# Two of the first four pairs of head groups by column tiles, and a planner with other transfer times

## The chip, the cores and the metric

The kernel runs on one core of one Trainium2 chip. The metric is the time of one execution on the device in microseconds, as the median of several runs; lower is better.

## The reference

Two layers, each of them attention with a compressive memory followed by a feed-forward network, on one sequence of 2048 tokens with 640 features. Both layers use the same weights. All inputs are bf16.

```python
x = x + attention(layernorm(x)); x = x + relu(layernorm(x) @ w1) @ w2      # twice, w1: 640 x 1728

def attention(x):                       # 32 heads of 20 features, 4 segments of 512 tokens
    q, k, v = x @ wq, x @ wk, x @ wv    # split into heads and segments
    M, z = 0, 0
    for s in range(4):
        a_dot = softmax(q_s k_s^T * 20**-0.5 + causal_mask) v_s
        a_mem = (phi(q_s) M) / (phi(q_s) z + 1e-6)      # phi(t) = t + 1 if t > 0 else exp(t)
        o_s = sigmoid(beta) * a_mem + (1 - sigmoid(beta)) * a_dot
        M, z = M + phi(k_s)^T v_s, z + sum(phi(k_s))
    return concat(o) @ wo
```

## The kernel before

The program is not written in the order in which it runs. `plan()` describes the work as generators ("streams"), each of which yields operations with a cost in ns, with what they wait for and with the buffer that they need. `Sched.run` places one operation after the other: it takes, among the heads of all streams, the one that can start first by the planner's own times (a delay called `late` can be added, and a priority settles ties). Each engine then gets its instructions as one fixed list, with waits on semaphores, and works through it in order. So a wrong time in the planner costs nothing by itself: it only makes an order in which an instruction stands ahead of others that could have run. `plan()` is built for each of several switch costs in `STARTS`, which differ by 0.75 ns, and the plan is taken whose order gives the smallest sum of four passes of `Sched.late`, a replay of the order in which transfers land late at random.

The numbers that the planner uses for transfers: an issue time, bytes divided by a rate, and a latency `lat` (`dma`, `ld`, `turn`, `late_loads`). `PE_MARGIN`, `TRUST_NS` and `JOIN_NS` are margins on waits of PE. `keep_busy` puts products with the identity (L627, "fillers") in front of an instruction where the planner expects PE to wait for long.

The work, by (layer `a`, segment `s`), eight times:

- `lnorm`/`ln_b`: statistics (L651) and normalization on DVE, the power -1/2 on POOL (L665), then a transpose by DMA (`turn`, L671, issued from SP's queue, which it holds while it is issued). The first segment is transposed on PE instead (L728).
- `proj_part`, `proj_v`: products for K, Q (into `stg`, feature by feature) and V (into `v_aug`, token by token, with a column of ones for each head).
- `spill`, `fill`: K and Q go to DRAM (`scr`) and come back as `pad`, four heads at partitions 0, 32, 64 and 96. For the first pair `first_heads` copies `stg` to `pad` directly.
- `scores` (L1103): a *pair* `m` is two groups of four heads; there are 32 pairs, four in each segment. Scores of four heads run in row tiles, in up to five rounds of two halves (the buffers X and Y). `exps` (L1155) turns them into `PT` on ACT, `causal` (L1167) clears above the diagonal on POOL.
- `apply`: the values of a pair, in one of two ways. *By token* (`values_by_token`, L1197): `PT` is the stationary operand and 21 columns of V move, 40 products for each group of four heads; DVE divides straight from PSUM (L1209, L1210, L1213) into `o_sb`. *By column tiles* (L1246): V is stationary in four column tiles and `PT` moves, 16 products for each group; the result is features by tokens, so it is evicted to `av` (L1254 on DVE or L1255 on ACT), transposed by DMA to `avt` (`turn_av`) and then divided (`divide`, L1282, L1283, L1290).
- `combine`, `turn_o`, `out_proj`: the memory's part is added, `o_sb` is transposed by DMA to `oT`, and `wo` is applied.
- `ffn`: 65 products of 512 columns with `w1`, then 112 products with `w2`, 320 columns wide.

Which pairs go by token is set here; four pairs make a segment, so this is pairs 0 to 3:

```python
BY_TOKEN = ((0, 0),)                               # segments
LATER = range(len(BY_TOKEN) * G // 2, NSEG * G)    # pairs that go through turn_av and divide
```

Of the kernel before, what the change touches and what calls it, by code (L numbers as in the profile page):

```python
# [14 lines left out]
NSEG = 4  # L15
# [3 lines left out]
FC = D // 128  # L19
# [138 lines left out]

LONE_NS = 300.0
SWITCH_NS = 97.0  # L160
STARTS = [SWITCH_NS + 0.75 * (k - 32 // 2) for k in range(32)]
LATE_NS = 300.0
JOIN_NS = 4000.0
SEM_NS = 60.0
PE_MARGIN = 80.0
IDLE_NS = 300.0
COLD_NS = 8000.0
TRUST_NS = {"dma": 1000.0, "pool": 400.0, "act": 400.0, "dve": 400.0, "pe": 0.0}
HOLDERS = 1
# [3 lines left out]
class Sched:  # L173
# [93 lines left out]
    def run(self):  # L267
        while True:
# [22 lines left out]
            for prio, n, st, alts, op, late in heads:  # L291
                ok = []
                if op.mode == "cols" and self.pe_mode == "full" and not self.streams[0][4]:
                    since = max([self.at(t) for t in op.waits], default=0.0)
                    late = max(0.0, JOIN_NS - max(0.0, alts[0][1] - since)) if alts else 0.0
                if prio > 0 and alts and alts[0][3] == "pe":
                    sl = self._pick(op.acq).tks if op.acq is not None else []
                    sure = max([self.at(t) + TRUST_NS[self.P.lane(t)] for t in op.waits + sl], default=0.0)
                    late = max(late, sure - alts[0][1])
                for end, start, k, e in alts:  # L300
                    if not any(p2 < min(prio, HOLDERS) and st2 is not st
                               and any(e2 == e and s2 + HOLD_TOL[e] < end for _, s2, _, e2 in al2[:1])
                               for p2, _, st2, al2, _, _ in heads):
# [31 lines left out]
            if op.dma is not None:  # L335
                tk = self.P.dma(e, fns[0][0], op.dma)
                self.dma_free = max(self.dma_free, start + 300.0) + tail[1]
                self.t[(id(tk[0]), tk[1])] = max(self.dma_free, end) + tail[0]
                if tail[2]:
                    self.free[e] = max(end, self.dma_free)  # L340
                out = tk
            else:
                marks = []
                for fn, mark in fns:
                    tk = self.P.op(e, fn, mark)
                    if tk is not None:
# [6 lines left out]
    def late(self, seed):  # L353

        rnd = random.Random(seed)
        free = {e: 800.0 for e in ENGS}
        t = {}
        dma_free = 0.0
        for e, hold, tail, waits, out, is_dma in self.log:
            m = SEM_NS + (PE_MARGIN if e == "pe" else 0.0)  # L360
            start = max([t[id(k[0]), k[1]] + m for k in waits], default=0.0)
            start = max(free[e], start)
            free[e] = start + hold
            if is_dma:
                dma_free = max(dma_free, start + 300.0) + tail[1]
                land = max(dma_free, free[e]) + tail[0] + rnd.expovariate(1.0 / LATE_NS)
                if tail[2]:
                    free[e] = max(free[e], dma_free)
            else:
                land = free[e] + tail  # L370
            for k in out:
                if k is not None:
                    t[id(k[0]), k[1]] = land
        return max(t.values())
# [33 lines left out]
def plan(switch, sb, sem_, psum, dram, A_x, A_wq, A_wk, A_wv, A_wo, A_beta, B_x, B_w1, B_w2, out):  # L408
# [84 lines left out]


    def ld(e, name, nbytes, fn, waits=()):
        tk = yield dma(e, sem_("d_" + name), nbytes, fn, waits, lat=2200.0)
        S.set(name, tks=[tk])

    def wload(e, name, w, src, waits=()):
# [24 lines left out]
    def late_loads():  # L524
# [27 lines left out]
        for n, (name, nbytes, fn) in enumerate(pieces):  # L552
            if name not in sems:
                sems[name] = sem_("d_" + name)
            w = yield Need("ex", *divmod(n, 5))
            if n == n2:
                v0 = yield Need("v00")
                q1 = yield Need("q01")
                w2w = v0 + q1 + early_done
            tk = yield dma("sp", sems[name], nbytes, fn, w[:1] + (w2w if n >= n2 else []) + z1, issue=400.0, lat=4500.0)  # L560
            left[name] -= 1
            if left[name] == 0:
                S.set(name, tks=[tk])
# [101 lines left out]
        tk = yield pool(760, lambda e: e.tensor_tensor(rstd[:, sl], lnU[:, sl], mhalf[:, 0:n], ALU.pow), [tk] + h)  # L665
        return tk

    def turn(slot_sem, dst, src, waits):

        n = src.shape[-1] // 128  # L670
        tk = yield dma("sp", slot_sem, 32768 * n, lambda e: e.dma_start_transpose(dst, src), waits,  # L671
                       issue=max(1400.0, 140.0 * n), lat=2000.0, rate=270.0, holds=True)
        return tk

    def lnorm(s, x_tks, pool_, parts=1):
# [3 lines left out]
        for p0 in range(0, 4, n):  # L679
# [11 lines left out]
            for i in range(p0, p0 + n, 2):  # L691
                t = 4 * s + i
                nm = lambda e, bx, t, k: e.tensor_scalar(
                    bx.ap[:, k * D:k * D + D], x_sb[:, t + k, :], mv[:, t + k, 0:1], rstd[:, t + k:t + k + 1],
                    ALU.subtract, ALU.mult)
                bx, t0 = yield dve(D, 4, lambda e, bx, t=t: nm(e, bx, t, 0), [tch], extra=120, acq=XN)
                t1 = yield dve(D, 4, lambda e, bx=bx, t=t: nm(e, bx, t, 1), [tch], extra=120)
                tT = yield from turn(xn_sem[id(bx)], xt.ap[:, i * FC:(i + 2) * FC, :], bx.ap, [t0, t1] + xt.tks)
                bx.release(tT)
                done.append(tT)  # L700
        return xt, done
# [474 lines left out]

        return 32 if (g, hh) != (G - 1, 3) else DH + 1

    BY_TOKEN = ((0, 0),)

    def values_by_token(m, a, s, g0, vt):

# [44 lines left out]
    def apply(m):  # L1227
# [30 lines left out]
        S.set("av", m, tks=[sl] + ev)  # L1258
        yield from done_values(a, s, g0, tk)

    LATER = range(len(BY_TOKEN) * G // 2, NSEG * G)

    def turn_av(m):
        ev = yield Need("av", m)
        sl, ev = ev[0], ev[1:]
        at = yield Acq([AVT])
        tT = yield from turn(avt_sem, at.ap, sl.ap.rearrange("p z t -> p (z t)"), ev + at.tks)
        sl.release(tT)
        S.set("avt", m, tks=[at, tT])

# [52 lines left out]
    def turn_o(a, s):  # L1323
        ow = yield Need("oseg", a, s)
        turned = []
        for k in range(2):
            ot = yield Acq([OT[k]])
            ot.users = []
            tT = yield from turn(ot_sem[id(ot)], ot.ap, o_sb[:, 2 * k:2 * k + 2, :].rearrange(
                "p i d -> p (i d)"), ow + ot.tks)  # L1330
            turned.append(tT)
            S.set("oT", a, s, k, tks=[ot, tT])
        OSB.release(*turned)
# [17 lines left out]
    def ln_b(p):  # L1351
        def f(a, s):
# [21 lines left out]
            tT = yield from turn(xn_sem[id(bx)], xt.ap[:, 2 * p * FC:(2 * p + 2) * FC, :], bx.ap, tn + xt.tks)  # L1374
            bx.release(tT)
            S.set("hx", a, s, p, tks=[tT])
        return f
# [188 lines left out]
```

## Time and profile before

| | |
|---|---|
| runs | 565.68, 567.0, 568.76 us; median 567.0 us |
| profiled execution | 565.3 us, of which the span of instructions is 563.5 us |
| granted clock of TensorE | 1.00 |
| values by token | 320 products (8 groups of 40) |
| values by column tiles | 896 products (56 groups of 16) |
| fillers (L627) | 66 products |
| transposes `avt<-av` | 28 |

In the rows of the profile, a *group* is line, engine, operation, what is written and read, shapes and count, then busy time, mean duration and idle time before. A row of the *timeline* is a start, a duration, the instruction with its count, and in brackets how long the engine had been idle and what ended that. Products overlap in PE's pipeline, so what one costs is the distance from its start to the next start and not its duration.

### The profile page before, as it was taken

What the parts mean: (1) busy time and instruction counts of PE and PEld (TensorE: products, weight loads), DVE (VectorE), ACT (ScalarE), POOL (GpSimd) and SP (SyncE); (2) the same over time, 40 slices, a digit from 0 to 9 for tenths busy, and PEclk for the clock granted to TensorE, in tenths of its full rate; (3) what the DMA queues carried; (4) which work ended last, traced back from release to release, by engine and by line L of the source; (5) the groups of instructions that cost most, each with busy time, mean ns of one, the idle gap of its engine ahead of it and who ended that gap; (6) DMA issues with size and microseconds to landing.
All of it is one profiled execution on the core that took longest, in us unless ns stands there. A gap on an engine that the chain in (4) does not pass through costs nothing.

```text
span 563.5 us, 12875 instructions
## 1 busy us (share of the span) xinstructions
PE 556.4 (99%) x5219; PEld 305.0 (54%) x5219; DVE 420.1 (75%) x1070; ACT 404.2 (72%) x512; POOL 195.1 (35%) x302
## 2 busy tenths in 40 slices
PE   8999999999999999999999999999999999999998
PEld 7664555445554454645446544555445654665655
DVE  6989789888999689878898997688747964560202
ACT  4789998987788878778986688778878678113140
POOL 4544344333344335444433443035322433110000
PEclk9999999999999999999999999999999999999999
DMA  8695988383474136542375131880326410512101
GB/s 268 120 221 138 238 218 182 74 224 56 97 171 94 44 88 159 118 95 72 92 163 115 27 66 26 193 148 20 67 80 173 109 43 20 116 45 48 47 1 47
DMA packets 130109, 60.93 MB, mean 108 GB/s; under 512 B 108930, under 2 KB 119938, under 8 KB 130050
## 3 DMA queue, kind: packets, MB, share of 16 engines
q1 hardware_dynamic: 129830, 59.85, 45.5%
q8 instruction: 41, 0.67, 0.5%
q10 hardware_dynamic: 220, 0.26, 0.2%
q14 instruction: 18, 0.15, 0.1%
HBM read 20.57 MB, written 12.85 MB: 59 GB/s over the span
## 4 chain that ended last, share of the span: by engine, by line
PE 87%; DVE 8%; DMA 2%; ACT 1%; SPq 1%; issue 0%
PE ps L643 56%; PE ps L640 11%; PE ps L1103 8%; PE ps L1246 6%; DVE stats L651 2%; PE ps L996 2%; PE ps L1197 1%; PE ps L1047 1%; DVE x_sb L1317 1%; PE ps L1394 1%; DMA avt<-av 1%; DVE xn_tok L705 1%; SPq L913 1%; DMA oT<-o_sb 1%; ACT PT L1155 1%; DVE stg L816 1%
## 5 line engine op out<-in xcount | busy, mean ns | idle before, releaser
L1155 ACT ACTIVATE PT<-ps 128x1024 bf16<-128x1024 f32 x320 | 310.0, 1022 | 70.3 <-PE ps L1103 64.6
L1167 POOL TENSOR_SCALAR_AFFINE_SELECT PT<-PT 128x512 bf16<-128x512 bf16 x256 | 166.6, 668 | 268.2 <-ACT PT L1155 267.9
L643 PE MATMUL ps<-w_r,hT 128*128 128x320 bf16 (+2 forms) x768 | 123.0, 299 | 0.0
L643 PE MATMUL ps<-xnT,w_r 128*128 128x512 bf16 x416 | 113.3, 379 | 0.0
L1317 DVE TENSOR_TENSOR x_sb<-x_sb,ps 128x320 bf16<-128x320 bf16 (+1 forms) x128 | 60.3, 479 | 66.7 <-PE ps L643 66.0
L643 PEld LDWEIGHTS ps<-w_r,hT 128*128 128x128 bf16 x768 | 72.4, 98 | 31.9 <-issue 4.4
L1425 ACT ACTIVATE hT<-ps 128x512 bf16<-128x512 f32 x55 | 32.7, 598 | 50.0 <-PE ps L643 49.7
L1103 PE MATMUL ps<-pad 20*128 20x128 bf16 (+3 forms) x1024 | 64.8, 301 | 1.6 <-ACT PT L1155 0.9
L643 PEld LDWEIGHTS ps<-xnT,w_r 128*128 128x128 bf16 x416 | 39.7, 98 | 44.0 <-issue 3.2
L651 DVE BATCH_NORM_STATS2 stats<-x_sb 128x6 f32<-128x320 bf16 x126 | 56.4, 472 | 2.1 <-DMA x_sb<-in_A_x_dram 1.8
L1254 DVE CAST av<-ps 128x512 bf16<-128x512 f32 x53 | 36.2, 684 | 14.8 <-PE ps L1246 14.7
L1103 PEld LDWEIGHTS ps<-pad 20*128 20x128 bf16 x1024 | 18.3, 92 | 52.6 <-ACT PT L1155 25.6
L643 PE MATMUL ps<-wo_r,oT 128*128 128x320 bf16 x256 | 46.1, 299 | 0.0
L1246 PE MATMUL ps<-PT,v_aug 128*32 128x256 bf16 (+5 forms) x896 | 40.7, 302 | 0.0
L1423 DVE TENSOR_SCALAR hT<-ps 128x512 bf16<-128x512 f32 x49 | 33.4, 683 | 9.1 <-PE ps L643 9.0
L640 PE MATMUL ps<-xnT,w_r 128*128 128x512 bf16 x104 | 39.6, 380 | 0.0
L643 PE MATMUL ps<-wv_r,xnT 128*128 128x320 bf16 x192 | 36.7, 300 | 0.0
L643 PE MATMUL ps<-xnT,wk_r 128*128 128x512 bf16 (+1 forms) x140 | 36.1, 349 | 0.0
L643 PE MATMUL ps<-xnT,wq_r 128*128 128x512 bf16 (+1 forms) x140 | 34.9, 349 | 0.0
L665 POOL TENSOR_TENSOR rstd<-lnU,mhalf 128x2 f32<-128x2 f32 (+2 forms) x25 | 20.8, 831 | 38.0 <-DVE lnU L661 34.4
L816 DVE CAST stg<-ps 128x512 bf16<-128x512 f32 (+1 forms) x48 | 29.5, 618 | 3.3 <-PE ps L643 3.2
L1290 DVE TENSOR_TENSOR o_sb<-avt,rden 128x320 bf16<-128x320 bf16 x56 | 30.5, 562 | 0.6
(117 smaller groups left out, 695.8 us busy)
## 6 DMA issues: line engine op xcount, KB each, us to landing
pad<-scr SPq DMA_DIRECT2D x124, 80.0 KB
scr<-stg SPq DMA_DIRECT2D x34, 256.0 KB, 2.9
out_dram<-x_sb SPq DMA_DIRECT2D x15, 160.0 KB, 1.8
w_r<-in_B_w_dram SPq DMA_DIRECT2D x10, 216.0 KB, 4.2
w_r<-in_B_w_dram SPq DMA_DIRECT2D x13, 160.0 KB, 2.8
x_sb<-in_A_x_dram SPq DMA_DIRECT2D x9, 160.0 KB, 2.8
scr<-w_r SPq DMA_DIRECT2D x5, 256.0 KB, 3.6
x_sb<-in_A_x_dram SPq DMA_DIRECT2D x3, 320.0 KB, 7.2
```

The costliest lines, as they stand in the source:

```text
L640: bk, tk = yield pe(mm_ns(n), [(lambda e, bk, a=a, b=b: e.matmul(bk.ap[:, 0:n] if len(b.shape) == 2 else bk.ap[:, 0:n].rearrange("p (i n) ...
L643: tk = yield pe(mm_ns(n), [(lambda e, k=k, a=a, b=b, bk=bk: e.matmul(bk.ap[:, 0:n] if len(b.shape) == 2 else bk.ap[:, 0:n].rearrange("p (i ...
L651: tk = yield dve(320, 1, lambda e, c2=c2: e.bn_stats(stats6[:, t, c2, :], x_sb[:, t, c2 * 320:(c2 + 1) * 320]), xt)
L816: te = yield evac(N, 1, lambda e, sg=sg, bk=bk: e.tensor_copy(sg.ap[:, t0:t0 + N], bk.ap[:, 0:N]), lambda e, sg=sg, bk=bk: e.activation(sg ...
L1103: fns.append([(lambda e, z=z, j=j, hh=hh, N=N, o=o, sl=sl: e.matmul(ps[:, hh, o:o + N], sl.ap[32 * hh:32 * hh + DH, z, 0, 128 * j:128 * j ...
L1155: tx = yield act(1024, lambda e, dst=dst, src=src: e.activation(dst, src, ACT.Exp, scale=SCALE), sc + pw)
L1167: tm = yield pool(600.0, lambda e, reg=reg: e.affine_select(out=reg, in_=reg, pattern=[[0, 4], [1, 128]], compare_op=ALU.is_ge, fill=0.0, ...
L1246: fns.append((lambda e, bk, j=j, hh=hh, pt=pt, g=g0 + z: e.matmul(bk.ap[32 * hh:32 * hh + wide(g, hh), 128 * j:L], VAUG[vx(a, s)][:, j].re ...
L1254: te = yield evac(L, 1, lambda e, sl=sl, z=z, bk=bk: e.tensor_copy(sl.ap[:, z], bk.ap), lambda e, sl=sl, z=z, bk=bk: e.activation(sl.ap[:, ...
L1317: ta = yield dve(n, 1, lambda e: e.tensor_tensor(x_sb[:, t, c0:c0 + n], x_sb[:, t, c0:c0 + n], bk.ap[:, 0:n], ALU.add), [tk] + list(waits) ...
L1423: th = yield evac(512, 1, lambda e, dc=dc, bk=bk: e.tensor_scalar(hT[:, dc, :], bk.ap[:, :], 0.0, None, ALU.max), lambda e, dc=dc, bk=bk: ...
L1425: lambda e, dc=dc, bk=bk: e.activation(hT[:, dc, :], bk.ap[:, :], ACT.Relu), [tk] + HT.tks)
```

## The change

Pairs 0 and 1 get their values by column tiles, pairs 2 and 3 stay by token. The planner's latencies are set for each transfer by itself; two margins are added: an operation on ACT or DVE that waits for a transfer is planned as if the transfer ended 800 ns later (`SURE_NS`), and transfers issued between 8 and 106 us are given 600 ns more (`EARLY_NS`). The replay that chooses among plans delays those transfers too and adds 1 us after a long wait of PE (`COOL_NS`), and 48 plans are built instead of 32. All lines after the constants move down by up to 11; the diff:

```diff
-STARTS = [SWITCH_NS + 0.75 * (k - 32 // 2) for k in range(32)]
+STARTS = [SWITCH_NS + 0.75 * (k - 48 // 2) for k in range(48)]
+SURE_NS = 800.0
+EARLY_NS = 600.0
+LOADS_NS = 106e3
+COOL_NS = 1000.0
...
@@ Sched.run
+                if alts and alts[0][3] in ("act", "dve"):
+                    sure = max([self.at(t) for t in op.waits if self.P.lane(t) == "dma"], default=0.0)
+                    late = max(late, sure + SURE_NS - alts[0][1])
...
-                self.t[(id(tk[0]), tk[1])] = max(self.dma_free, end) + tail[0]
+                self.t[(id(tk[0]), tk[1])] = max(self.dma_free, end) + tail[0] + (EARLY_NS if 8e3 < start < LOADS_NS else 0.0)
@@ Sched.late
+            if e == 'pe' and start - free[e] > 800.0 and start > 10e3:
+                start += COOL_NS
...
+                if 8e3 < start < LOADS_NS:
+                    land += rnd.expovariate(1.0 / EARLY_NS)
@@ plan
-        tk = yield dma(e, sem_("d_" + name), nbytes, fn, waits, lat=2200.0)
+        tk = yield dma(e, sem_("d_" + name), nbytes, fn, waits, lat={"x0a": 1950.0, "x0b": 1950.0, "x01": 1500.0, "wk0": 2900.0, "wq0": 2900.0, "wk1": 2900.0, "wq1": 2500.0, "wv": 2200.0, "x10": 3800.0, "x11": 3800.0}.get(name, 2200.0))
...
-            tk = yield dma("sp", sems[name], nbytes, fn, w[:1] + (w2w if n >= n2 else []) + z1, issue=400.0, lat=4500.0)
+            tk = yield dma("sp", sems[name], nbytes, fn, w[:1] + (w2w if n >= n2 else []) + z1, issue=400.0, lat=3500.0)
...
-    def turn(slot_sem, dst, src, waits):
+    def turn(slot_sem, dst, src, waits, lat=2000.0):
...
-                       issue=max(1400.0, 140.0 * n), lat=2000.0, rate=270.0, holds=True)
+                       issue=max(1400.0, 140.0 * n), lat=lat, rate=270.0, holds=True)
...
-    BY_TOKEN = ((0, 0),)
+    BY_TOKEN = (2,3)
...
-        if (a, s) in BY_TOKEN:
+        if m in BY_TOKEN:
...
-    LATER = range(len(BY_TOKEN) * G // 2, NSEG * G)
+    LATER = [m for m in range(NSEG * G) if m not in BY_TOKEN]
...
@@ turn_av: lat=1600.0;  turn_o, lnorm and ln_b: lat=2400.0
```

More of the change, by code (lines that the diff above doesn't have):

```diff
@@ L697, in lnorm @@
                 t1 = yield dve(D, 4, lambda e, bx=bx, t=t: nm(e, bx, t, 1), [tch], extra=120)
-                tT = yield from turn(xn_sem[id(bx)], xt.ap[:, i * FC:(i + 2) * FC, :], bx.ap, [t0, t1] + xt.tks)
+                tT = yield from turn(xn_sem[id(bx)], xt.ap[:, i * FC:(i + 2) * FC, :], bx.ap, [t0, t1] + xt.tks, lat=2400.0)
                 bx.release(tT)
@@ L1266, in turn_av @@
         at = yield Acq([AVT])
-        tT = yield from turn(avt_sem, at.ap, sl.ap.rearrange("p z t -> p (z t)"), ev + at.tks)
+        tT = yield from turn(avt_sem, at.ap, sl.ap.rearrange("p z t -> p (z t)"), ev + at.tks, lat=1600.0)
         sl.release(tT)
@@ L1329, in turn_o @@
             tT = yield from turn(ot_sem[id(ot)], ot.ap, o_sb[:, 2 * k:2 * k + 2, :].rearrange(
-                "p i d -> p (i d)"), ow + ot.tks)
+                "p i d -> p (i d)"), ow + ot.tks, lat=2400.0)
             turned.append(tT)
@@ L1373, in f @@
                 tn.append(tk)
-            tT = yield from turn(xn_sem[id(bx)], xt.ap[:, 2 * p * FC:(2 * p + 2) * FC, :], bx.ap, tn + xt.tks)
+            tT = yield from turn(xn_sem[id(bx)], xt.ap[:, 2 * p * FC:(2 * p + 2) * FC, :], bx.ap, tn + xt.tks, lat=2400.0)
             bx.release(tT)
```

## The prediction

> **What bounds the kernel now.** I read the page first, for the engine that is busy for the whole span:
>
> ```profile
> span 563.5 us, 12875 instructions
> PE 556.4 (99%) x5219; PEld 305.0 (54%) x5219; DVE 420.1 (75%) x1070; ACT 404.2 (72%) x512; POOL 195.1 (35%) x302
> PEclk9999999999999999999999999999999999999999
> ```
>
> PE is busy 99% of the span, at one clock throughout. But a busy PE can be a waiting one, so I read PE's timeline next, for the distance from one start to the next in dense stretches and for bracketed idle time.
>
> ```profile
> 8.04 1.00 PE L627 MATMUL ps<-ident 128*128 128x128 bf16 x15
> 8.88 0.27 PE L640 MATMUL ps<-xnT,wk_r 128*128 128x256 bf16 x1
> 8.98 0.60 PE L643 MATMUL ps<-xnT,wk_r 128*128 128x256 bf16 x4
> 9.42 0.44 PE L728 MATMUL ps<-ident,xn_tok 128*128 128x128 bf16 x5
> 9.70 0.27 PE L640 MATMUL ps<-xnT,wq_r 128*128 128x256 bf16 x1
> ...
> 18.41 0.27 PE L640 MATMUL ps<-xnT,wk_r 128*128 128x256 bf16 x1
> 19.30 0.40 PE L1103 MATMUL ps<-pad 20*128 20x512 bf16 x4 [0.62 <-DMA pad<-stg]
> ...
> 84.00 0.31 PE L640 MATMUL ps<-wo_r,oT 128*128 128x320 bf16 x1 [0.21 <-DMA oT<-o_sb]
> ...
> 94.88 0.39 PE L1103 MATMUL ps<-pad 20*128 20x512 bf16 x2 [0.27 <-ACT PT L1155]
> 99.50 0.40 PE L1103 MATMUL ps<-pad 20*128 20x512 bf16 x4 [0.20 <-ACT PT L1155]
> 100.11 0.31 PE L640 MATMUL ps<-wv_r,xnT 128*128 128x320 bf16 x1 [0.22 <-DVE av L1254]
> 166.41 0.40 PE L1103 MATMUL ps<-pad 20*128 20x384 bf16 x8 [0.44 <-ACT PT L1155]
> 195.96 0.34 PE L996 MATMUL ps<-BD,stg 128*128 128x84 bf16 x3 [0.23 <-DVE om_sb L1007]
> 555.48 1.79 PE L643 MATMUL ps<-w_r,hT 128*128 128x320 bf16 x12
> 557.11 0.30 PE L643 MATMUL ps<-w_u,hL 128*128 128x320 bf16 x1
> ```
>
> The last two rows are the pace when nothing is in the way: 12 products 320 wide in 557.11 - 555.48 = 1.63 us, 0.136 us each. Five 256 wide take 9.42 - 8.88 = 0.54 us, 0.109 each. The bracketed waits shown are the larger ones after the start; together 0.62 + 0.21 + 0.27 + 0.20 + 0.22 + 0.44 + 0.23 = 2.19 us. So PE is bound by its own list of instructions. A change can win what it takes off that list and about 2 us of waits; it loses what its new order makes PE wait.
>
> **The change part by part.**
>
> *Values of pairs 0 and 1.* Four groups of 40 narrow products (two pairs of two head groups) become four groups of 16 products in column tiles. Both kinds are in the trace, and so is a burst of scores:
>
> ```profile
> 28.62 1.16 PE L1197 MATMUL ps<-w_r,PT 128*128 128x21 bf16 x40
> 29.64 0.30 PE L640 MATMUL ps<-wv_r,hT 128*128 128x320 bf16 x1
> ...
> 96.30 0.30 PE L640 MATMUL ps<-wv_r,xnT 128*128 128x320 bf16 x1
> 96.43 0.71 PE L643 MATMUL ps<-wv_r,xnT 128*128 128x320 bf16 x4
> 97.07 0.40 PE L1103 MATMUL ps<-pad 20*128 20x384 bf16 x8
> 97.40 0.73 PE L1246 MATMUL ps<-PT,v_aug 128*32 128x512 bf16 x16
> 98.06 0.34 PE L996 MATMUL ps<-BD,w_r 128*128 128x84 bf16 x3
> ```
>
> By token: 29.64 - 28.62 = 1.02 us a group. By column tiles: 98.06 - 97.40 = 0.66. Removed 4 x 1.02 = 4.08, added 4 x 0.66 = 2.64: -1.44 us, all on PE's path.
>
> *Leaving the full array.* From 96.30 to 97.07 lie five products that need 5 x 0.136 = 0.68, so going over to scores costs 0.09 us; what coming back costs is inside the 0.33 of the burst (97.40 - 97.07). In the changed order of instructions PE leaves full-array work 173 times instead of 169: +4 x 0.09 = +0.36. The same number of score products (1024) is issued in 164 bursts instead of 162: +2 x 0.33 = +0.65.
>
> *The start.* Fillers (the products with the identity) are 54 instead of 66, all 12 of them taken from the first 9 us; the other 39 stay fillers, in other places. That alone is worth nothing, because the start is paced by the normalization and by transfers:
>
> ```profile
> 6.46 0.88 DVE L651 BATCH_NORM_STATS2 stats<-x_sb 128x6 f32<-128x320 bf16 x2
> 7.26 0.43 DVE L705 TENSOR_SCALAR xn_tok<-x_sb,mv,rstd 128x640 bf16<-128x640 bf16 x1
> ```
>
> A pair of statistics takes 7.26 - 6.46 = 0.80 us of DVE. In the new order one half of the fourth tile's statistics, 0.40 us, moves ahead of the second tile's `lnU`, from which that tile's normalization (7.26 today) follows by way of POOL; another half moves out from behind, so I put it 0.2 us later, at most 0.4. PE then transposes all four tiles ahead of its first K product; today the last two transposes, 2 x (9.70 - 9.42) = 0.56 us, stand behind it. The first K product therefore starts about 0.6 us after today's 8.88 with 0.56 us of work done earlier: both orders are level there, to within 0.2. The first scores wait today for `pad` until 19.30, after 0.62 us of idle. The transfers that fill it are issued in the same order behind the same evictions, so I keep 19.30. In front of the first scores the old order has 51 products of K and Q and 25 of V, the new one 55 and 27: 4 x 0.109 + 2 x 0.136 = 0.71 us more real work is done by then, in the time that was idle. -0.71 us; if `pad` comes 0.2 later, because its evictions slide with that, the gain is 0.5, and if they slide by the 0.6 of the first K product it is 0.1.
>
> *DVE and ACT.* The busy times of PE, PEld, DVE, ACT and POOL from 40 to 60 us, and the groups with their mean durations:
>
> ```profile
> 40.00:60.00 20.00, 20.00 (x243) 10.18 (x242) 19.93 (x54) 18.32 (x24) 8.68 (x13) 1.00 0.63 154
> ```
>
> ```profile
> L1209 DVE RECIPROCAL rden<-ps 128x16 f32<-128x16 f32 x8 | 2.0, 250 | 1.0 <-PE ps L1197 1.0
> L1210 DVE TENSOR_TENSOR rden<-rden,omg 128x16 f32<-128x16 f32 x8 | 2.2, 270 | 0.1
> L1213 DVE TENSOR_TENSOR o_sb<-ps,rden 128x320 bf16<-128x320 f32 x8 | 3.9, 485 | 0.1
> L1254 DVE CAST av<-ps 128x512 bf16<-128x512 f32 x53 | 36.2, 684 | 14.8 <-PE ps L1246 14.7
> L1282 DVE RECIPROCAL rden<-avt 128x32 f32<-128x32 bf16 x28 | 9.6, 342 | 6.7 <-DMA avt<-av 6.7
> L1283 DVE TENSOR_TENSOR rden<-rden,omg 128x32 f32<-128x32 f32 x28 | 8.3, 296 | 0.5
> L1290 DVE TENSOR_TENSOR o_sb<-avt,rden 128x320 bf16<-128x320 bf16 x56 | 30.5, 562 | 0.6
> ```
>
> A pair by token costs DVE 2 x (0.250 + 0.270 + 0.485) = 2.01 us, by column tiles 2 x 0.684 + 0.342 + 0.296 + 2 x 0.562 = 3.13. Two pairs: +2.24 us, around the stretch shown, where DVE is busy 19.93 of 20 us. I cost this at nothing, since PE still has K, Q and V products of two segments to put in front of a late eviction, and since 10 evictions of 512 columns move from DVE to ACT over the whole span (DVE's 46 become 36 in the new order); without that cover it is up to +2.24.
>
> *The queue of SP.* Two more transposes `avt<-av` are issued, and they wait in SP's queue for the eviction of `av`. Queued behind the first are the second turn of `phk`, five loads of `wo` and the first spill of segment (0,1); behind the second, two spills, a turn of `phk` and the fills for pair 4.
>
> ```profile
> 55.27 1.86 SPq L934 DMA_DIRECT2D pad<-scr  x4
> ...
> 72.77 0.39 PE L1103 MATMUL ps<-pad 20*128 20x384 bf16 x6
> ...
> 80.10 3.16 SPq L671 DMA_TRANSPOSE oT<-o_sb  x2
> ```
>
> The fills for pair 4 are issued at 55.27 today and its first scores are in the burst at 72.77: 15 us of cover, against two issues of some 1.3 us. Cost nothing. The end of segment (0,0) isn't touched by this: its last two pairs stay by token, so `o_sb` needs no second transpose in front of `oT` (80.10 today). In the new order the last values of pair 3 stand about 1 us earlier among PE's work (the sum of the distances up to them), which covers the 0.21 us wait at 84.00.
>
> *The new costs of transfers and the margins* add no instruction; they only move them. Waits after the start of 2.19 - 0.62 = 1.57 us can go or be matched by others. I take -0.48: the one at 84.00 (0.21) and a fifth of the other 1.36, since a new order of 5,000 products has misfits of its own. Bounds: -1.57, and up to what the slower rival below costs.
>
> Sum: -1.44 + 0.36 + 0.65 - 0.71 - 0.48 = -1.62 us. The profiled execution took 565.3 us, 1.8 more than its span; it would take 563.7. The three timed runs lie above it (565.68, 567.0, 568.76; median 567.0), so the median after is 567.0 - 1.62 = 565.4. A change of 0.5%, 2.8 us, is about what a measurement of this kernel can tell from none; the forecast is half of that.
>
> **The rivals.**
>
> *More waits go.* All 1.57 us of later waits vanish, and with margins on what follows transfers the runs no longer spread 3 us (568.76 - 565.68) but sit near the profiled one, 1.7 us under the median. For it: five of the waits shown end with ACT or DVE, which the margin is about. Against: the margin is for work behind a transfer, and none of those five ends with one. Time: 567.0 - 1.14 - 1.57 - 0.8 (half of 1.7) = 563.5, -0.6%. Chance 0.34.
>
> *Slower: DVE stalls on the transposed values of pair 1.* DVE's instructions run in order, and the reciprocal L1282 waits for `avt` (sum, times, longest; then the time from issue to landing):
>
> ```profile
> DVE rden L1282 <- DMA avt<-av: 6.7, 5, 1.6
> ```
>
> ```profile
> DMA to landing us min/median/max: 2.7/2.8/4.5
> ```
>
> Five of 28 such waits took 6.7 us, the longest 1.6. In the new order ten DVE instructions stand between pair 1's last eviction and its reciprocal; at 20 us for 54 (the row of 40 to 60 us) that is 3.7 us. A landing after the median 2.8 fits, one after 4.5 does not. Behind it stand the evictions of V and Q banks that PE needs, on the engine with 0.07 us to spare. Price: 2.24 + 2 x 1.6 = 5.4 us, less the sum's 1.6: 570.8. It decides once more than 4.4 us of it reach PE. TensorEngine Tiling (the Trainium skill, Performance Considerations, PSUM Bottleneck) says that tiling speeds up PE and not the eviction of PSUM, which may become the bottleneck; by that rule it would be this rival, and the full DVE of 40 to 60 us agrees so far, while PE, busy 20.00 of 20.00 in that stretch, speaks against. Chance 0.20.
>
> *It does not matter.* The start gives 0.1 instead of 0.71, no wait goes and one of 0.5 us appears: 567.0 - 1.62 + 0.61 + 0.48 + 0.5 = 567.0. It belongs to the forecast's class.
>
> **How the numbers follow.** The forecast has 0.30 and the last case, which ends within 0.5% too, 0.16; more waits gone 0.34, slower 0.20. The forecast's own range with the last case is 564.2 to 568.5. Though more waits gone has a slightly higher chance than the forecast alone, the two cases within 0.5% together have 0.46, and the predicted time is theirs. The range takes in the first rival with the rest of the spread (563.5 less about 2) and the slower one up to half of its price (567.0 - 1.6 + 2.7 = 568.1, and 1 us for the spread): 561.5 to 569.1. Faster by over 0.5%: 0.34; within: 0.46; slower: 0.20.
>
> **What would show it.** In the profile after: 160 products L1197's kind and 960 in column tiles; the first scores near 19.3 us with less idle time before them; first `oT` product near 83 instead of 84.00; a span about 1.6 us shorter. Wrong, if DVE's waits for `avt` grow by more than 2 us and PE shows bracketed waits between 50 and 60 us, or if PE's bracketed waits after 20 us sum to less than 0.5 us or over 4.

## The result, and the profile after

The changed kernel takes 562.76 us (median of 562.46 to 562.98), the kernel before 566.74 us on the same chip: ratio 0.9934, 95% interval 0.9914 to 0.9954. It is faster by 0.66%, 3.98 us, and the interval leaves out no change. The forecast was 565.4 us, a gain of 1.6 us, and its likeliest class "within 0.5%"; what came is nearest to the rival "more waits go" (563.5 us). The profiled execution took 562.46 us (565.3 before), with a span of 560.6 (563.5). All line numbers after the constants are higher by up to 11.

The changed kernel's engines, from its page, and its granted clock, from the view of the cores (its page has no row of the clock):

```profile
span 560.6 us, 12651 instructions
PE 555.5 (99%) x5110; PEld 302.6 (54%) x5111; DVE 410.8 (73%) x1060; ACT 409.7 (73%) x522; POOL 194.3 (35%) x302
core 0: 560.6 us, clock 1.000
```

PE's timeline of the changed kernel at the places that the prediction showed (start, duration, instruction, in brackets the idle time before it):

```profile
9.71 0.27 PE L651 MATMUL ps<-xnT,wk_r 128*128 128x256 bf16 x1
...
19.24 0.30 PE L654 MATMUL ps<-wv_r,xnT 128*128 128x320 bf16 x1
19.47 0.40 PE L1114 MATMUL ps<-pad 20*128 20x512 bf16 x4
...
80.36 0.34 PE L1007 MATMUL ps<-BD,w_r 128*128 128x84 bf16 x3 [0.27 <-DVE om_sb L1018]
...
83.48 0.31 PE L651 MATMUL ps<-wo_r,oT 128*128 128x320 bf16 x1
...
100.47 0.31 PE L651 MATMUL ps<-wv_r,xnT 128*128 128x320 bf16 x1 [0.25 <-DVE av L1265]
```

PE starts its first scores without the 0.62 us of idle time, and the first product with `oT` without its 0.21. After 20 us only the two bracketed waits are left, 0.52 us, where the six that the prediction added up came to 1.57. One of the two, for `av` near 100 us, was there before; the other, 0.27 us at 80.36, is new. The groups of the changed kernel that answer to the part on DVE, and its waits for `avt`:

```profile
L1265 DVE CAST av<-ps 128x512 bf16<-128x512 f32 x56 | 38.3, 684 | 12.9 <-PE ps L1257 12.5
L1208 PE MATMUL ps<-w_r,PT 128*128 128x21 bf16 x160 | 4.8, 172 | 0.0
```

```profile
DVE rden L1293 <- DMA avt<-av: 1.8, 4, 0.7
```

```profile
40.00:60.00 20.00, 20.00 (x213) 10.20 (x211) 17.84 (x48) 18.99 (x26) 8.27 (x13) 1.00 1.00 219
```

The first two of these transfers, for pairs 0 and 1, took the longest from issue to landing (the stretch of 37 to 58 us):

```profile
DMA to landing us min/median/max: 4.8/4.9/5.0
```

DVE's waits for `avt` fell from 6.7 us to 1.8, and between 40 and 60 us it is busy 17.84 us instead of 19.93. Evictions of K and Q, 512 columns wide, went to ACT: DVE does nine of them in this stretch before (5.9 us, L816) and four after (2.7 us, L827), and ACT is busy 18.99 us instead of 18.32.

**List and lag.** To separate work from waiting in all kernels alike, I laid PE's instructions end to end in their order, each at the start-to-start distance that the prediction uses (0.136 us for a product 320 wide, 0.66 for a column group, 1.02 for a group by token, 0.33 for a burst of scores, 0.09 for leaving the full array, and so on). The start of the last product on this list is the *list*; how much later it started in the trace is the *lag*. Before: 549.35 + 11.64 = 560.99 us, the last product's start. After: 548.19 + 9.87 = 558.06. So the last start came 2.93 us earlier: 1.16 is work off the list and 1.77 is less lag. The list is an estimate that uses the same distances for every kernel, so the differences between kernels say more than the lags themselves. And list, lag and idle time are read from the one execution that was profiled, which lay from 1.5 us under to 2.3 us over the median of its kernel (e4 and e2); a difference in lag of about 2 us between two kernels can be a difference between executions.

### The profile page after: what moved, and what is told of

It reads as the page before. It is cut to its first block, busy times and chain, and to the rows that moved or that the text cites. A ratio compares the mean times of both kernels' runs of the same rounds, so it can differ in the third digit from the quotient of the medians.

```text
span 560.6 us, 12651 instructions
## 1 busy us (share of the span) xinstructions
PE 555.5 (99%) x5110; PEld 302.6 (54%) x5111; DVE 410.8 (73%) x1060; ACT 409.7 (73%) x522; POOL 194.3 (35%) x302
## 4 chain that ended last, share of the span: by engine, by line
PE 90%; DVE 8%; DMA 1%; ACT 0%; POOL 0%; issue 0%
PE ps L654 58%; PE ps L651 12%; PE ps L1114 9%; PE ps L1257 7%; DVE stats L662 2%; PE ps L1058 2%; PE ps L1007 2%; DVE x_sb L1328 1%; PE ps L1405 1%; DVE stg L827 1%; DMA x_sb<-in_A_x_dram 1%; DVE xn_tok L704 1%; DVE av L1265 0%; DVE xn_tok L716 0%; DVE mv L664 0%; ACT PT L1166 0%
## 5 line engine op out<-in xcount | busy, mean ns | idle before, releaser
L1114 PE MATMUL ps<-pad 20*128 20x384 bf16 (+3 forms) x1024 | 64.9, 301 | 0.0
L1265 DVE CAST av<-ps 128x512 bf16<-128x512 f32 x56 | 38.3, 684 | 12.9 <-PE ps L1257 12.5
L1301 DVE TENSOR_TENSOR o_sb<-avt,rden 128x320 bf16<-128x320 bf16 x60 | 33.3, 572 | 0.7
L654 PEld LDWEIGHTS ps<-wo_r,oT 128*128 128x128 bf16 x256 | 24.8, 98 | 11.3 <-issue 1.3
```

Of the source, the lines that this page charges most:

```text
L654: tk = yield pe(mm_ns(n), [(lambda e, k=k, a=a, b=b, bk=bk: e.matmul(bk.ap[:, 0:n] if len(b.shape) == 2 else bk.ap[:, 0:n].rearrange("p (i ...
L1114: fns.append([(lambda e, z=z, j=j, hh=hh, N=N, o=o, sl=sl: e.matmul(ps[:, hh, o:o + N], sl.ap[32 * hh:32 * hh + DH, z, 0, 128 * j:128 * j ...
L1265: te = yield evac(L, 1, lambda e, sl=sl, z=z, bk=bk: e.tensor_copy(sl.ap[:, z], bk.ap), lambda e, sl=sl, z=z, bk=bk: e.activation(sl.ap[:, ...
L1301: to = yield dve(320, 1, lambda e, dst=dst, src=src, rz=rz: e.tensor_tensor(dst, src, rz, ALU.mult), [tg] + OSB.tks)
```

## The experiments

In each, `STARTS` holds only the one switch cost of the order that was run; with e3, e10 and e11 this is one that the replay placed behind its first, and with e12 one that is not among the planner's 48. The first four ran beside the kernel before at 565.92 us (median), e5 to e8 at 566.16, e9 to e12 at 566.47; ratios are to these, so that they compare across the groups better than medians do.

| kernel | pairs by token | transfer times | margins | PE idle, 20 to 75 us | list | lag | median us | ratio |
|---|---|---|---|---|---|---|---|---|
| before | 0 to 3 | old | no | 0.06 | 549.35 | 11.64 | 566.74 | 1 |
| e11 | 0 to 3 | old | no | 0.09 | 549.78 | 14.06 | 568.44 | 1.0029 |
| e2 | 0 to 3 | new | yes | 0.63 | 550.00 | 17.49 | 569.51 | 1.0072 |
| e1 | 2, 3 | old | no | 2.57 | 548.20 | 20.66 | 571.12 | 1.0084 |
| e7 | 2, 3 | new | no | 1.29 | 548.69 | 19.26 | 571.84 | 1.0098 |
| e10 | 2, 3 | new | no | 1.20 | 547.92 | 14.22 | 568.25 | 1.0024 |
| e8 | 2, 3 | old | yes | 1.09 | 547.88 | 12.24 | 564.29 | 0.9963 |
| **after** | 2, 3 | new | yes | 0.00 | 548.19 | 9.87 | 562.76 | 0.9934 |
| e3 | 2, 3 | new | yes | 0.33 | 549.19 | 18.39 | 572.61 | 1.0120 |
| e9 | 2, 3 | new | yes, 900 ns | 0.13 | 548.23 | 12.27 | 565.56 | 0.9975 |
| e6 | 3 | new | yes | 0.42 | 547.06 | 13.23 | 564.90 | 0.9972 |
| e12 | 3 | new | yes | 0.42 | 547.00 | 14.39 | 565.21 | 0.9978 |

**e1_cols_only.** The column tiles alone, in the kernel before with its own planner.

```diff
-    BY_TOKEN = ((0, 0),)
+    BY_TOKEN = (2, 3)
-        if (a, s) in BY_TOKEN:
+        if m in BY_TOKEN:
-    LATER = range(len(BY_TOKEN) * G // 2, NSEG * G)
+    LATER = [m for m in range(NSEG * G) if m not in BY_TOKEN]
```

> The kernel before with one thing changed: pairs 0 and 1 get their values by column tiles; latencies, margins and the number of plans stay as they were (the plan chosen is fixed). Counted as in the prediction, PE's list is 1.1 us shorter than before's. Theory A (the list is shorter by the column tiles, and the rest of the gain comes from transfers that are planned with the right times and margins): -1.1 us from the list, waits and spread between runs as before: about 565.5 us, ratio 0.998. Theory B (any new order of the column tiles does it; the planner's constants do nothing): about 563 us, ratio 0.993, with the runs within 1 us of each other. Theory C (pairs 0 and 1 need the right transfer times, or DVE waits for the transposed values): 568 or more.

571.12 us, ratio 1.0084 (1.0070 to 1.0098). PE's list shrank by 1.15 us as counted, but the lag grew by 9.0. In PE's waits after 20 us of e1 (sum, times, longest) the transfers lead, of which the kernel before had 0.2 us:

```profile
PE ps L640 <- DMA xnT<-xn_tok: 1.7, 2, 1.4
PE ps L640 <- DMA hT<-xn_tok: 1.5, 1, 1.5
```

```profile
57.99 0.31 PE L640 MATMUL ps<-wv_r,hT 128*128 128x320 bf16 x1 [1.51 <-DMA hT<-xn_tok]
```

In stretches of e1 around that wait (PE, PEld, DVE, ACT, POOL busy; the column before the last two is the granted clock's, followed by the share of DMA and GB/s):

```profile
56.00:58.00 2.00, 0.49 (x6) 0.10 (x3) 1.73 (x3) 2.00 (x3) 1.64 (x3) 1.00 0.84 186
58.00:60.00 2.00, 2.00 (x53) 1.68 (x53) 0.60 (x2) 0.71 (x2) 0.38 (x1) 1.00 1.15 161
60.00:62.00 2.00, 2.00 (x16) 1.15 (x9) 1.52 (x7) 1.78 (x2) 0.00 (x0) 0.56 1.05 254
62.00:64.00 2.00, 2.00 (x10) 0.74 (x9) 1.13 (x4) 0.69 (x2) 1.27 (x2) 0.59 1.59 155
```

Two microseconds after the wait the clock is granted at 0.56 and 0.59 for 2 us each: another 2 x 0.44 + 2 x 0.41 = 1.70 us lost. The fall of the clock is not what makes e1 slow: three of its five executions had a mean clock of 1.000 and took 569.97 to 571.18 us. The column tiles do what the sum says to PE's list, and in the one order that was drawn for them alone the kernel is slower.

**e2_plan_only.** The planner's side alone: the changed kernel with pairs 0 to 3 by token.

```diff
-    BY_TOKEN = (2,3)
+    BY_TOKEN = (0, 1, 2, 3)
```

> The changed kernel with all four first pairs by token, as before; the new latencies, margins and 48 plans stay (the plan chosen is fixed). PE's list is 0.6 us longer than before's. Theory A: +0.6 from the list, -1.8 from waits and about -1 from the spread between runs: about 564.5 us, ratio 0.996, runs within 1 us. Theory B: +0.6 and nothing else: 567.3, ratio 1.001. Theory D (the order is a lottery: each new plan has waits of its own, whatever the constants): anywhere from 564 to 570.

569.51 us, 1.0072 (1.0053 to 1.0092). At 150 us on the list its lag is 7.36 us, under that of before (8.41) and of after (7.56). By 200 it has grown by 5.2, most of it at one place; PE's timeline and the stretches around it, of e2:

```profile
168.26 0.38 PE L651 MATMUL ps<-xnT,w_r 128*128 128x512 bf16 x1 [2.17 <-issue]
```

```profile
168.00:170.00 2.00, 1.74 (x5) 0.68 (x6) 0.65 (x2) 0.92 (x2) 0.64 (x1) 0.64 1.05 335
170.00:172.00 2.00, 2.00 (x6) 0.61 (x4) 1.35 (x3) 0.00 (x0) 0.00 (x0) 0.51 0.08 31
```

A wait of 2.17 us, and then 2 x 0.36 + 2 x 0.49 = 1.70 us of clock. The profile puts the wait down to "issue", but the times name a transfer. The product at 168.26 reads `xnT`, and the second of the two transposes that fill it was issued at 161.26 and took 6.9 us to land, until 168.17; the first took 3.9 (its issue, and the time from issue to landing of the two):

```profile
161.26 1.35 SPq L682 DMA_TRANSPOSE xnT<-xn_tok  x1
```

```profile
DMA to landing us min/median/max: 3.9/5.4/6.9
```

It was issued after 106 us, where `EARLY_NS` adds nothing. The profiled execution (571.82 us) lies 2.3 us over the median: five of the six executions had a mean clock of 1.000, and they took 568.86 to 572.11 us. So neither half of the change gives the gain, in the one order drawn for each.

**e3_after_2nd_plan.** The changed kernel in the order that its replay ranked second.

```diff
-STARTS = [SWITCH_NS + 0.75 * (k - 48 // 2) for k in range(48)]
+STARTS = [SWITCH_NS + 0.75 * (k - 48 // 2) for k in (15,)]
```

> The changed kernel with another of its 48 plans: the switch cost of the plan that the replay ranks second. PE's list is 1.0 us longer than that of the changed kernel, most of it fillers (75 instead of 54). Theory A: the same constants give the same few waits: 562.8 + 1.0 = 563.8, runs within 1 us. Theory D: waits of its own, 2 us or more away from 563.8.

572.61 us, 1.0120 (1.0103 to 1.0137): with no other edit, 9.9 us slower than the changed kernel. Between 70 and 100 us on the list its lag grows by 5.4 us where the changed kernel's grows by 1.5; its timeline and its stretches there:

```profile
83.02 0.34 PE L1007 MATMUL ps<-BD,w_r 128*128 128x84 bf16 x3 [1.62 <-DVE w_r L975]
```

```profile
82.00:84.00 2.00, 0.98 (x13) 0.48 (x17) 1.97 (x7) 0.47 (x2) 0.69 (x2) 1.00 1.02 202
84.00:86.00 2.00, 1.83 (x29) 0.77 (x18) 1.46 (x5) 2.00 (x3) 0.64 (x1) 0.81 1.17 125
86.00:88.00 2.00, 2.00 (x9) 1.15 (x8) 0.69 (x2) 1.58 (x3) 0.86 (x2) 0.50 0.72 161
...
88.00:90.00 2.00, 2.00 (x15) 1.02 (x14) 0.82 (x2) 0.64 (x1) 0.36 (x1) 0.83 1.00 151
```

The clock takes 2 x (0.19 + 0.50 + 0.17) = 1.72 us of it. The switch cost that the planner assumes differs by 11.25 ns between the two orders. Which of such orders is taken is worth more here than the whole change.

**e4_no_fillers.** The changed kernel in its own order, without the fillers after 10 us.

```diff
-        if gap < IDLE_NS or self.idle_fn is None:
+        if gap < IDLE_NS or self.idle_fn is None or start > 10e3:
```

> The changed kernel in the same order, without the 39 fillers that stand after the first 10 us. PE's list is 2.7 us shorter by the count. As the prediction has it (fillers stand where PE would wait anyway): no difference, 562.8 us, and 2 us more of bracketed waits of PE. Rival (fillers are planned longer than the waits are and hold up what comes behind them): up to 2.7 us faster, 560.1. Third: PE's clock or its start after a wait is slower without them: above 563.5.

565.9 us, 0.9991 (0.9980 to 1.0002), that is 3.1 us slower than the changed kernel by medians and 564.43 - 562.46 = 2.0 by profiled executions. The list fell by 2.67 us (548.19 to 545.52), the lag rose by 4.64. In e4 PE does the same product as before it at the same time, with a longer wait in front of it, and then the clock falls:

```profile
80.36 0.34 PE L1007 MATMUL ps<-BD,w_r 128*128 128x84 bf16 x3 [1.02 <-DVE om_sb L1018]
...
83.06 0.40 PE L1114 MATMUL ps<-pad 20*128 20x384 bf16 x8 [0.57 <-ACT PT L1166]
```

```profile
80.00:82.00 2.00, 1.33 (x23) 0.68 (x23) 1.93 (x7) 1.66 (x3) 1.59 (x3) 1.00 1.09 229
82.00:84.00 2.00, 1.43 (x26) 0.66 (x15) 1.93 (x7) 2.00 (x4) 0.65 (x2) 0.85 1.22 214
84.00:86.00 2.00, 2.00 (x9) 1.10 (x8) 1.07 (x3) 1.94 (x3) 0.51 (x1) 0.50 1.94 165
86.00:88.00 2.00, 2.00 (x14) 1.02 (x13) 1.19 (x3) 0.37 (x1) 0.72 (x2) 0.79 0.54 130
```

The clock takes 2 x (0.15 + 0.50 + 0.21) = 1.72 us. Between 75 and 85 us the work that PE waits for sets the pace (`om_sb` on DVE is the releaser in both kernels, at the same 80.36), so the fillers there cost nothing; without them the clock is lost. In six of the twelve executions of e4 the mean clock was 0.997, as one such fall would give, and in the other six 0.994, as two would; the profiled one is of the first kind, which is why the medians lie further apart than the profiled executions.

**e5_by_token_twice.** Each product by token of the changed kernel issued twice, the order unchanged (the same at the second place where `fns` is issued).

```diff
-                        tk = yield pe(25.2 * len(fns), fns)
+                        tk = yield pe(25.2 * len(fns), [(f, False) for f, _ in fns] + fns)
```

> The changed kernel, its order unchanged, but each product by token of pairs 2 and 3 is issued twice (the second overwrites the first with the same values): 160 more products of 32 columns on PE, which by the row of the changed kernel's products by token (25 to 26 ns apart in a burst) put 160 x 25.8 ns = 4.1 us on PE's list, all of it between about 30 and 110 us; nothing else moves. Theory A (PE's list is the bound, everywhere in the stretch): +4.1 us, 566.9 (566.3 to 567.5), ratio to the kernel before about 1.0015. Theory B (these products stand where PE would wait anyway, so work put there is partly free): +1 to +3 us, 563.8 to 565.8, and the sum of idle time before PE falls by what is missing. Theory C (a later PE makes DVE and the transfers late in turn): over +5 us, above 567.8.

566.49 us, 1.0006 (0.9995 to 1.0018), so 3.7 us above the changed kernel's median. The list grew by 4.13 us, the lag fell by 0.36, and the last product starts 3.77 us later (561.83 against 558.06). Work put on PE's list in this stretch appears in the time to about nine tenths (by the two ratios to the kernel before, 1.0006 and 0.9934, to all of it): PE's list is the bound there, as the prediction had it.

**e6_one_pair_by_token.** Pair 2 goes by column tiles too.

```diff
-    BY_TOKEN = (2,3)
+    BY_TOKEN = (3,)
```

> The change taken one step further: pair 2 goes by column tiles too and only pair 3 by token, in an order that the changed planner draws for it. PE's list, by the durations of the two traces: two groups by token of 1.02 us become two by columns of 0.66 (-0.72), with 3 fillers fewer and 1 mode change more, -1.15 us in all. Theory A (list alone, waits as in the changed kernel): 561.6 (561.2 to 562.0). Theory D (the order that is drawn sets the waits, and orders drawn so far came out 3 to 9 us apart): anything from 561 to 573, and with four of six orders slower than the kernel before, over 565.9 is likelier than not; the difference from 561.6 should then be seen whole as waits or as a granted clock under 1.0 and not as work on PE's list.

564.90 us, 0.9972 (0.9961 to 0.9983): faster than before, 2.1 us slower than the changed kernel. The list is 1.13 us shorter, the lag 3.36 longer, without a clock under 1.0.

**e7_no_margins** and **e8_old_transfer_times.** The planner's change split: new transfer times without margins, and margins with the old transfer times (the three calls of `turn` with `lat=2400.0` lose it as the one shown loses its own).

```diff
 e7
-SURE_NS = 800.0
-EARLY_NS = 600.0
+SURE_NS = -1e9
+EARLY_NS = 0.0
-COOL_NS = 1000.0
+COOL_NS = 0.0
-                    land += rnd.expovariate(1.0 / EARLY_NS)
+                    land += 0.0
 e8
-        tk = yield dma(e, sem_("d_" + name), nbytes, fn, waits, lat={"x0a": 1950.0, "x0b": 1950.0, "x01": 1500.0, "wk0": 2900.0, "wq0": 2900.0, "wk1": 2900.0, "wq1": 2500.0, "wv": 2200.0, "x10": 3800.0, "x11": 3800.0}.get(name, 2200.0))
+        tk = yield dma(e, sem_("d_" + name), nbytes, fn, waits, lat=2200.0)
-            tk = yield dma("sp", sems[name], nbytes, fn, w[:1] + (w2w if n >= n2 else []) + z1, issue=400.0, lat=3500.0)
+            tk = yield dma("sp", sems[name], nbytes, fn, w[:1] + (w2w if n >= n2 else []) + z1, issue=400.0, lat=4500.0)
-        tT = yield from turn(avt_sem, at.ap, sl.ap.rearrange("p z t -> p (z t)"), ev + at.tks, lat=1600.0)
+        tT = yield from turn(avt_sem, at.ap, sl.ap.rearrange("p z t -> p (z t)"), ev + at.tks)
...
```

> The changed kernel with the new transfer times but without the margins: SURE_NS, EARLY_NS and COOL_NS take no effect, and the order is drawn anew. PE's list +0.5 us (7 fillers more, 1 mode change more). Theory M (the margins are what keeps PE from waiting for transfers): waits of PE that end with a DMA come back, 2 to 4 us in all after 20 us, with what the clock loses on top; 566 to 572. Theory D (a lottery among orders; margins don't matter of themselves): no more DMA-ended waits than in the changed kernel (under 0.5 us), and a time that may be 563.2 (list alone) or later for other reasons.

> The changed kernel with its margins but with the old transfer times in the planner (2200 ns for all first loads, 4500 for the weights, 2000 for every turn), the order drawn anew. PE's list -0.3 us; before the first scores it places 27 fillers as the kernel before does, where the changed kernel places 15, so the first scores come about 0.7 us later than at 19.47. Theory T (the new transfer times bring the gain): back to 565 to 569, with DMA-ended waits where the old times are too short (the turns of xn_tok and oT, taken as 2.0 us where the traces show landings of 2.4 and more). Theory M (the margins bring it): 562.5 to 563.5. Theory D: neither is told by the waits of PE that end with a DMA.

e7: 571.84 us, 1.0098 (1.0078 to 1.0119). e8: 564.29 us, 0.9963 (0.9948 to 0.9978). PE's waits after 20 us that end with a transfer are 1.2 us in e7 and 0.5 in e8 (none in the changed kernel), fewer than theory M had asked of e7. Where the loads and the column tiles are, the stretches of 20 to 75 us show it better; e1, e7, e8, the changed kernel, in this order:

```profile
20.00:75.00 55.00, 52.43 (x572) 29.90 (x570) 46.23 (x118) 47.56 (x63) 21.22 (x32) 0.97 0.89 194
```

```profile
20.00:75.00 55.00, 53.71 (x571) 29.46 (x569) 51.15 (x135) 49.24 (x66) 21.63 (x32) 1.00 0.90 201
```

```profile
20.00:75.00 55.00, 53.91 (x571) 29.27 (x570) 49.76 (x135) 49.36 (x65) 22.12 (x32) 1.00 0.92 196
```

```profile
20.00:75.00 55.00, 55.00 (x578) 29.59 (x576) 50.06 (x133) 52.69 (x71) 22.63 (x34) 1.00 0.91 209
```

PE's idle time is 55.00 less its busy time: 2.57, 1.29, 1.09, 0.00.

**e9_margin_900, e10_no_margins_2nd_order, e11_before_2nd_order, e12_one_pair_2nd_order.** More orders: a larger margin in the planner; e7, the kernel before and e6 with another order.

```diff
 e9
-EARLY_NS = 600.0
+EARLY_NS, PLAN_EARLY = 600.0, 900.0
-                self.t[(id(tk[0]), tk[1])] = max(self.dma_free, end) + tail[0] + (EARLY_NS if 8e3 < start < LOADS_NS else 0.0)
+                self.t[(id(tk[0]), tk[1])] = max(self.dma_free, end) + tail[0] + (PLAN_EARLY if 8e3 < start < LOADS_NS else 0.0)
 e10: e7's edits, with
+STARTS = [SWITCH_NS + 0.75 * (k - 48 // 2) for k in (1,)]
 e11: the kernel before, with
+STARTS = [SWITCH_NS + 0.75 * (k - 32 // 2) for k in (0,)]
 e12: e6's edit, with
+STARTS = [104.625000]
```

> The changed kernel with one planner constant moved: a transfer issued between 8 and 106 us is taken to land 900 ns later instead of 600 (EARLY_NS in _place alone), and the order is drawn anew with it. PE's list +0.03 us (5 fillers more, one score burst fewer, 1 mode change more): 548.2, as the changed kernel. Theory M (a margin keeps PE's work away from transfers that land late, and more of it does so more): no wait of PE after 20 us ends with a DMA, the excess over the list at the end is 9.0 to 10, and the time 562.2 to 563.2. Theory D (each order is a draw of its own whatever the margin): 562 to 572, likeliest around 566.

565.56 us, 0.9975 (0.9963 to 0.9987): same list, 2.4 us more lag, and one wait of 0.7 us for a transfer. In this order more margin did not mean less waiting.

> As the experiment without margins (571.84), but with another of the 48 orders that its planner draws (the second of them instead of the fourth). PE's list 547.9, 0.8 us shorter than there and 0.3 shorter than the changed kernel's. Theory M (without margins PE waits for transfers and for what follows on them, in any order): excess at the end again over 13, time over 566. Theory D (that order was merely a bad draw): excess about 10, time 562.5 to 564.

568.25 us, 1.0024 (1.0011 to 1.0037), as theory M had it: lag 14.22. It is also 3.6 us faster than e7, so the order counts beside the margin.

> The kernel before with another of the 32 orders that its own planner draws (the first instead of the second); nothing else is changed. PE's list 549.74, 0.43 us longer than before's 549.31. Theory D (orders of one planner lie some us apart): excess elsewhere than 11.6, a time off 566.6 by more than 1 us, 568 to 572 by the other orders seen so far without margins (571.1 and 571.8). If the planner's choice matters little, 566.2 to 567.0.

568.44 us, 1.0029 (1.0017 to 1.0040): the kernel before, in another order, loses 2.4 us of lag and 0.43 of list.

> Pair 3 alone by token, as in the experiment that took 564.90, with another order of the changed planner (another supposed cost of a mode change, 104.6 ns). PE's list 546.95, 1.2 us shorter than the changed kernel's and as short as there. Theory A (list and waits of the changed kernel): 561.5. Theory M (with margins most orders have an excess of 10 to 13.3, as three of five so far): 561.6 to 565. Theory D without any hold by margins: 561 to 573.

565.21 us, 0.9978 (0.9968 to 0.9988): the shortest list of the table, lag 14.39. None of the orders tried beats the changed kernel.

**What follows from them together.** Up to 75 us there is a pattern, though it rests on one to five orders of each kind. With column tiles for pairs 0 and 1, PE idles 2.57 us between 20 and 75 us with the old planner, 1.29 and 1.20 with the new times alone, 1.09 with the margins alone, and 0.00 to 0.42 with both (five orders). By token it idles 0.06 and 0.09 with the old planner and 0.63 with the new one; the kernel before and e2:

```profile
20.00:75.00 55.00, 54.94 (x669) 32.02 (x668) 48.70 (x130) 50.66 (x68) 22.67 (x35) 1.00 0.82 193
```

```profile
20.00:75.00 55.00, 54.37 (x664) 31.92 (x662) 48.96 (x136) 49.58 (x66) 24.22 (x35) 1.00 0.87 190
```

In these orders the planner's change is therefore no gain of its own there: it pays for the column tiles, which need it. Behind 75 us there is none that these runs show: the lag grows by 4.1 us in the changed kernel from list position 70 to the end, by 6.1 in e9, 6.9 and 7.4 in e6 and e12, 11.1 in e2 and 12.2 in e3, all with both parts of the planner's change; by 6.0 and 8.0 in the two orders of the kernel before. On the margins the whole times lean one way (with column tiles, five of six orders with margins are faster than the kernel before, and none of three without), but they are few orders and they overlap: e3, with margins, is the slowest of all.

## Why the prediction was right and wrong

- *PE's list bounds the kernel:* right; e5 put 4.13 us on it and 3.7 to 3.8 came out.
- *Column tiles, leaving the full array, bursts, start (-1.44, +0.36, +0.65, -0.71: -1.14 in all):* right. The list is shorter by 1.16 us. That is counted with the prediction's own distances and so tests the counts alone; the distances are tested by the lag. Through the stretch with all four changed groups it is that of before: 5.37 us in both kernels at list position 20, 5.69 and 5.76 at 70. Were one of these terms wrong by some tenths, the lags would part there, unless another made up for it. (2 x 0.33 for the bursts is 0.66 and not 0.65.) The first scores came at 19.47 for 19.30 forecast, the first K product at 9.71 for 9.5.
- *DVE costed at nothing, because PE has other work in front of late evictions:* right, and the cover was not even needed: the rival with stalls on `avt` is refuted (waits 1.8 us instead of 6.7, PE busy 20.00 of 20.00 from 40 to 60 us). Long landings did come: those of pairs 0 and 1 took 5.0 and 4.8 us. DVE waited nothing for the first and 0.7 for the second, where the rival had 1.6 for each of two waits.
- *First `oT` product near 83:* right, 83.48 and no wait.
- *Waits, -0.48:* this is the step that failed, in size. The lag fell by 1.77 us: 0.87 between list positions 70 and 100, 0.91 between 150 and 200, the rest cancels. The bracketed waits of PE after 20 us give 1.05 of it (1.57 to 0.52); the other 0.7 us has no row of its own. The forecast took a fifth of the waits with ACT and DVE; four of those five went, the fifth, for `av`, stayed, and one of 0.27 us was new. What is left, 0.52 us, lies just above the 0.5 under which the prediction would have called itself wrong.
- *Why they went:* the rival named the margins. For the waits at 166.41 and 195.96 it cannot be `EARLY_NS`, which ends at 106 us, and no transfer ends either wait; `SURE_NS` holds over the whole plan. But margins alone do not do it: with both parts of the planner's change five other orders (e2, e3, e6, e12, and e9 with the larger margin) grew 0.9 to 5.2 us of lag between list positions 150 and 200, where the changed kernel grew 0.3. That it lost so little there is a matter of the order that was taken. Why this order has no misfit behind 110 us stays open.
- *From the profiled execution to the median:* the forecast moved both by the same, and that was off by 1.1 us. The profiled times fell by 2.84 us, the medians by 3.98, because the profiled run of before lay 1.4 under its median and that of after 0.3 under. A smaller spread is not shown by that: the changed kernel has four runs, and e5, in the same order, spread from 566.13 to 568.23.
- *The slower side:* it had 0.20, for DVE. The runs show a larger danger that the prediction did not price: an order with one hole in it. All eleven other orders of the table are slower than the changed kernel, by 1.5 to 9.9 us by their medians, six of them with a list within 1.0 us of its (for e8, the nearest, the intervals of the two ratios overlap), and each half of the change alone, in the order drawn for it, is slower than the kernel before. That the change came out at 3.98 us and not at the 1.1 us of its list is in part the luck of the order.

## What to carry to other kernels

When an order is drawn by a planner, count the change of the bound engine's list from the instructions themselves; here -1.14 us was forecast and -1.16 found, and the lag did not part while the changed work ran. But hold the forecast of the waits as wide as two orders of the *same* kernel differ (here 0.3, 2.0, 3.6 and 9.9 us in four pairs), and measure two or three orders before a gain of 1 us is put down to the edit. Put filler work where PE waits for others anyway: here it cost nothing there and kept the clock.

## What the runs showed of the hardware

A hole in PE's work can cost a second time. After a wait of 1.51 us (e1), of 2.17 us (e2), of 1.62 us (e3), and of 1.02 and 0.57 us within 3 us (e4), the granted clock fell, to 0.50 to 0.56 in its lowest stretch of 2 us, and the loss summed over the stretches is 1.70, 1.70, 1.72 and 1.72 us: the same each time, as 3.4 us at half the clock would give. TensorE: Matmul & The Clock Gate (the Trainium skill, Part 1, What's actually happening) has the clock at half after an idle window of about 3.4 us, in windows that run freely. The length and the half agree with these runs; that PE must idle for a whole such window does not, since its longest idle time was 2.17 us and in e4 it was busy in more than half of each 2 us shown. Nor does idle time alone decide: e7 idled 2.1 us between 80 and 88 us, in waits of up to 0.91 us, at a clock of 1.00, in these stretches of it:

```profile
80.00:82.00 2.00, 1.09 (x16) 0.58 (x14) 2.00 (x7) 1.17 (x2) 0.76 (x2) 1.00 0.99 308
82.00:84.00 2.00, 1.69 (x22) 0.97 (x22) 2.00 (x7) 2.00 (x3) 0.46 (x1) 1.00 1.16 167
84.00:86.00 2.00, 1.62 (x25) 0.78 (x25) 1.93 (x6) 2.00 (x3) 1.56 (x3) 1.00 1.19 242
86.00:88.00 2.00, 1.49 (x18) 0.87 (x19) 1.83 (x6) 0.79 (x2) 0.47 (x1) 1.00 1.33 130
```

And e1 kept a clock of 1.00 through a single wait of 1.38 us, longer than those of e4:

```profile
181.68 0.31 PE L640 MATMUL ps<-wv_r,xnT 128*128 128x320 bf16 x1 [1.38 <-DMA xnT<-xn_tok]
```

```profile
182.00:184.00 2.00, 2.00 (x22) 1.10 (x21) 0.92 (x4) 1.23 (x2) 0.20 (x1) 1.00 0.71 158
```

The traces' records of the granted clock show more than the stretches. Each of the four falls lasts 3.41 us at 0.50, and each begins a whole number of such lengths after the clock had come up: 16 in e1, 48 in e2, 23 in e3 and in e4. So in these runs the clock changes on a grid of 3.41 us that does not start anew at a wait, which also fits that one order loses the clock in some executions only (two of five in e1, one of six in e2, all of e3 and e4). I summed for each length of this grid the products that start in it, at 0.136 us for 320 columns, and counted a product that uses a quarter or a half of the array (scores, column tiles) for that share. The four lengths ahead of the falls have the four smallest sums of all 1751 (up to 552 us, in the 11 traces that have such records): 0.92 us in e2, 1.16 in e3, 1.39 in e1 and 1.44 in e4. The next is 1.52, and there the clock stayed. So it was thin work for the whole array in one such length, and not idle time by itself, that went with a fall. This is an estimate: there are four falls, and the weights were chosen after the fact.
